# Half-width first gate/up blocks, paired scores and a separate last projection in an attention and gated-unit kernel

## The chip, the cores and the metric

The kernel runs on one core of one Trainium2 chip. The metric is the device time in microseconds of one execution. The core has a matrix engine (TensorE, PE in the profile), a vector engine (DVE), an activation engine (ACT), a general engine (POOL) and SP, which here issues DMAs. Each takes its instructions in order and waits on semaphores. Weight loads of TensorE stand apart as PEld.

## The reference

Everything works on 2048 tokens of width 512 and is in bfloat16. With `xn` the layer norm of `x`:

```python
s = _A_ref(xn, A_k_cache, A_v_cache, A_wq, A_wo)   # 32 heads of 128, 2048 keys, softmax, output projection
g = _silu(_B_ref(xn, B_W_gate, B_W_up, B_W_down))  # relu(gate) * up, inner width 1792, then down to 512
return x + s * g
```

Per head the attention is `q = xn @ wq`, `p = softmax(q k^T / sqrt(128))`, `o = p v`; the heads' outputs, side by side, go through `wo` (4096 to 512).

## The kernel before, in words

Tokens are cut into four quarters Q of 512 (QB = 4) and 16 tiles n of 128 (NT). The head of the kernel normalises the first quarter by hand (`head_ln`): statistics of four tiles on DVE, square root on ACT, norms of tiles 0 and 1 on POOL and of 2 and 3 on DVE, then TensorE transposes each tile into PSUM (`head_transpose`), and ACT (three) and DVE (one) copy them into `xnT`. Before that, twelve dummy matmuls on a zero tile run on TensorE. The first weights, 256 columns of gate and of up, come in SP's queue and ACT's queue; the later ones in SP's.

The gated unit follows by quarters (`emit_gate_up`, `emit_down`): for each of 14 column blocks fc of 128, four gate matmuls and four up matmuls of 512 columns, a relu on ACT (L432), a product on DVE (L438); then the down projection, whose gate value lands in `g_sb`. During the first quarter DVE, POOL and SP normalise and transpose the other quarters (`ln_task`).

PSUM has a ring of three slots of two banks (`ps_r`, `ring_acquire`) and two banks of accumulators (`ps_acc`). `ring_acquire` makes TensorE wait until the slot's last readers are done.

The long part is attention. A block b is one head and one quarter: 128 blocks of 8 pairs. A pair is 2 tiles of 128 keys. For each pair TensorE makes two score matmuls (L582) into one ring slot, ACT takes the exponential of both (L592) into `PT`, and three pairs later (LAG) TensorE multiplies with the values, eight matmuls of 129 columns (L675), the last column being the softmax's sum. At a block's end DVE takes reciprocals (L605) and scales (L612), and SP transposes the result by DMA into `OT_store` (L627). At the first block of each group of four heads, DVE waits for all transposes of the group before (L603).

The order of TensorE's work is written out by hand in a dictionary `plan`. It gives steps of the pair loop extra tiles: at the first pair of a block the query projection of the next head (L515, four matmuls) and one tile of the output projection of the group before (L536, four matmuls); in the last four blocks, which have no next head, two tiles at the first and fifth pair. Steps without extra tiles run score, four values, score, four values. Steps with them run both scores, the extra tiles, eight values.

The last group's projection (`emit_final_tile`, L709) multiplies with the gate on DVE (L717), adds to `x` (L722) and stores. Its tiles for quarters 0 and 1 are in the plan of blocks 126 and 127. After the loop come the four of quarter 2, then the last block's output, which TensorE transposes and ACT copies (L647, L652), then the four of quarter 3.

Of the kernel before, what the change touches and what calls it, by code (L numbers as in the profile page):

```python
# [5 lines left out]
BF16 = mybir.dt.bfloat16  # L6
# [45 lines left out]
def bass_recurrent_scan__mha_block_cached__glu_gated_reglu__prompt_kernel(  # L52
# [51 lines left out]
    with ExitStack() as es:  # L104
# [60 lines left out]
        sem_tl = [newsem(16) for _ in range(QB)]  # L165
        sem_ptr = newsem()
        sem_otc = newsem()
# [29 lines left out]
        with nc.Block() as block:  # L197

            @block.tensor
            def _(_pe_eng):  # L200
# [13 lines left out]
                FCS = [0, min(2, FC), min(8, FC), FC]  # L214
# [24 lines left out]
                load_w(act, Wu_sb, wu_src, sem_wu, 0)  # L239
# [103 lines left out]
                def head_transpose(n, ntok, eng, sem):  # L343
                    tp_ps = ps_r[:, n, :].bitcast(BF16)
# [13 lines left out]
                    ring_tok[n // 2].append(ctok)  # L358

                def head_ln():  # L360
                    st = ln_stats(0)
                    st = ln_stats(1)
                    sq01 = ln_aggr([0, 1], st)
                    st = ln_stats(2)
                    c01 = ln_coef([0, 1], sq01)
                    n0 = ln_norm(pool, sem_nm, 0, c01)
                    n1 = ln_norm(pool, sem_nm, 1, c01)
                    st = ln_stats(3)
                    sq23 = ln_aggr([2, 3], st)
                    c23 = ln_coef([2, 3], sq23)  # L370
                    n2 = ln_norm(dve, sem_ln4, 2, c23)
                    n3 = ln_norm(dve, sem_ln4, 3, c23)
                    head_transpose(0, n0, act, sem_xa)
                    head_transpose(1, n1, act, sem_xa)
                    head_transpose(2, n2, act, sem_xa)
                    head_transpose(3, n3, dve, sem_xt)

# [27 lines left out]

                def emit_gate_up(Q):
                    qs = slice(Q * NQ, (Q + 1) * NQ)
                    par = Q % 2
                    h_tok = None
                    for fc in range(FC):  # L410
                        fs = slice(fc * 128, (fc + 1) * 128)
                        s = ring_acquire()
# [16 lines left out]
                        gk = fc % NSLOT  # L429
                        _wait(act, gtok)  # L430
                        _wait(act, gr_free[gk])
                        rtok = sem_relu.sig(act.activation(gr_sb[gk][:], ps_r[:, gb, :], ACTF.Relu))  # L432
                        _wait(dve, gu_tok)
                        _wait(dve, rtok)
                        if fc == 0:
                            _wait(dve, hT_free[par])
                        h_tok = sem_h.sig(
                            dve.tensor_tensor(hT[par][:, fc, :], gr_sb[gk][:], ps_r[:, gb + 1, :], ALU.mult)  # L438
                        )
                        gr_free[gk] = h_tok  # L440
                        ring_tok[s] = [rtok, h_tok]
                        if Q == 0:
                            ln_task(fc)
# [33 lines left out]
                for _i in range(12):  # L477
                    pe.matmul(ps_acc[:, 0, 0:D], warm[:, 0:128], warm[:], start=True, stop=True)
                head_ln()
                ring_cnt[0] = 2  # L480
# [17 lines left out]
                opg_tok = {}  # L498
                def blk_of(gp):
                    b, p = divmod(gp, NP)  # L500
                    h, Q = divmod(b, QB)
                    return b, h, Q, p

                def emit_M(items):
                    s = ring_acquire()
                    toks = [fn(*args, 2 * s + k) for k, (fn, *args) in enumerate(items)]
                    ring_tok[s] = toks
# [59 lines left out]
                s_slot = {}  # L567

                def open_S_pair(gp):
                    b, h, Q, p = blk_of(gp)  # L570
                    if p == 0:
                        _wait(pe, qt_ready[(h, Q)])
                        if Q == 0:
                            _wait(pe, kt_tok(h))
                    s_slot[gp] = ring_acquire()

                def emit_S_tile(gp, tt):
                    b, h, Q, p = blk_of(gp)
                    qs = slice(Q * NQ, (Q + 1) * NQ)
                    s = s_slot[gp]  # L580
                    t = 2 * p + tt
                    ins = pe.matmul(ps_r[:, 2 * s + tt, :], KT_sb[h % 2][:, t * 128:(t + 1) * 128],  # L582
                                    QT_sb[h % 2][:, qs], start=True, stop=True)
                    if tt == 0:
                        return
# [11 lines left out]
                def emit_norm_bank(b, bank, pvtok):  # L597
# [19 lines left out]
                    if b == NBLK - 1:  # L617
                        emit_last_transposes(hh, Q, ob, bank, tok)
                        return tok
# [3 lines left out]
                    tsem = sem_t[g % 2] if g < NG - 1 else sem_tl[Q]  # L623
                    for jj in range(2):
                        j = 2 * bank + jj
                        tsem.sig(
# [7 lines left out]
                last_ot = {}  # L634

                def emit_last_transposes(hh, Q, ob, bank, tok):
                    pending_last.append((hh, Q, ob, bank, tok))

                def flush_last_transposes():
                    s = ring_acquire()  # L640
                    for k, (hh, Q, ob, bank, tok) in enumerate(pending_last):
                        tp_ps = ps_r[:, 2 * s + k, :].bitcast(BF16)
                        _wait(pe, tok)
                        ins = None
                        for jj in range(2):
                            j = 2 * bank + jj
                            ins = pe.transpose(tp_ps[:, jj * 128:(jj + 1) * 128], Onorm[ob][:, j, :], ident[:])  # L647
                        ptok = sem_ptr.sig(ins)
                        _wait(act, ptok)
                        c0 = Q * NQ + bank * 256  # L650
                        last_ot[bank] = sem_otc.sig(
                            act.copy(OT_store[(NG - 1) % 2][:, hh, c0:c0 + 256], tp_ps[:, 0:256])  # L652
                        )
                    ring_tok[s] = list(last_ot.values())

                pending_last = []

                def emit_PV_tile(gp, tt):
# [3 lines left out]
                    if tt == 0:  # L662
                        if p == 0:
                            if gp == 0:
                                _wait(pe, tok_pool)
                            if Q == 0:
                                _wait(pe, v_tok(h))
                        pe.wait_ge(sem_exp.h, gp + 1)
                    t = 2 * p + tt
                    for j in range(4):  # L670
                        bank = j // 2
                        if t == 0 and j % 2 == 0:
                            _wait(pe, norm_tok[b - 1][bank] if b >= 1 else acc_free[bank])
                        o_ap = ps_acc[:, bank, (j % 2) * 256:(j % 2) * 256 + VW]
                        ins = pe.matmul(o_ap, PT[pb][:, tt, j * 128:(j + 1) * 128], V_sb[vb][:, t, :],  # L675
                                        start=(t == 0 and j % 2 == 0), stop=(t == KT - 1 and j % 2 == 1))
                        if t == KT - 1 and j == 1:
                            tx = sem_pv.sig(ins)
                        if t == KT - 1 and j == 3:
                            ty = sem_pv.sig(ins)  # L680
                    if t == KT - 1:
# [5 lines left out]
                        norm_tok[b] = (ntx, nty)  # L687

# [4 lines left out]

                NFT = len(fin_tmp)
                fin_free = [None] * NFT
                fin_cnt = [0]
                gL = NG - 1

                def emit_final_tile(n, bank):
                    Q, j = divmod(n, 4)  # L700
                    if n == 0:
                        _wait(pe, wo_tok(gL))
                    if j == 0:
                        _wait(pe, (sem_tl[Q], sem_tl[Q].n))
                    if Q == QB - 1:
                        _wait(pe, last_ot[j // 2])
                    ins = None
                    for hh in range(G):
# [3 lines left out]
                    fb = fin_cnt[0] % NFT  # L712
                    fin_cnt[0] += 1
                    _wait(dve, otok)
                    _wait(dve, fin_free[fb])
                    mtok = sem_opa.sig(
                        dve.tensor_tensor(fin_tmp[fb][:], ps_r[:, bank, 0:D], g_sb[:, n, :], ALU.mult))  # L717
                    _wait(dve, mtok)
                    if n == 0:
                        _wait(dve, base_done[NT - 1])  # L720
                    ftok = sem_opa.sig(
                        dve.tensor_tensor(x_sb[:, n, :], x_sb[:, n, :], fin_tmp[fb][:], ALU.add))  # L722
                    fin_free[fb] = ftok
                    if Q == QB - 1 or j % 2 == 1:
                        n0 = n if Q == QB - 1 else n - 1
                        _wait(sp, ftok)
                        sem_out.sig(sp.dma_start(out_t[:, n0:n + 1, :], x_sb[:, n0:n + 1, :]))
                    return mtok

                plan = {}  # L730
                for b in range(NBLK):
# [82 lines left out]
```

## Time and profile before

| what | value |
|---|---|
| median of 3 runs | 1299.38 us (1299.02 to 1300.44) |
| profiled execution, its own time | 1300.44 us |
| its span | 1298.6 us |
| TensorE busy | 1287.6 us |
| ACT busy | 1001.6 us |
| DVE busy | 442.5 us |
| DMA moved | 71.69 MB, 55 GB/s on average |
| exponentials (L592) | 1024, 952.5 us busy |
| value matmuls (L675) | 8192, 784.2 us busy |
| score matmuls (L582) | 2048, 755.1 us busy |

Busy time is the union of the instructions' durations. A matmul's duration holds the time in which its last column drains through the array, so neighbours overlap; how often matmuls start says more than how long each lasts. The span is from the first to the last instruction of the profiled execution, and its own time has 1.8 us around it.

### The profile page before, as it was taken

Reading aid. Unit: us, or ns where it says so; the run is one execution under the profiler, and the core shown is the slowest. Engines: PE = TensorE matmul, PEld = TensorE weight load, DVE = VectorE, ACT = ScalarE, POOL = GpSimd, SP = SyncE. Lnnn points to the kernel's source line nnn. Section 1 sums busy time; section 2 is a strip of 40 time slices with the busy share of each in tenths; the row PEclk is TensorE's granted clock in tenths of the full one; section 3 lists DMA queues with packets and bytes.
Section 4 is the critical chain, followed back from the end, with each engine's and each line's share of the span. In section 5 each row is a group of like instructions: output and inputs, shape, how many; then the busy total and the mean of one; then the engine's idle time right before and its main releaser. Section 6 shows DMA issues by size and latency. Waiting matters only on the chain.

```text
span 1298.6 us, 27683 instructions
## 1 busy us (share of the span) xinstructions
PE 1287.6 (99%) x11968; PEld 835.3 (64%) x11968; DVE 442.5 (34%) x1190; ACT 1001.6 (77%) x1109; POOL 11.5 (1%) x23
## 2 busy tenths in 40 slices
PE   9999999999999999999999999999999999999998
PEld 4444466666666666666666666666666666666665
DVE  6333322222323323323323323323323322334456
ACT  3322399888888888888888888888888888888884
POOL 2000000000000000000000000000000000000000
PEclk9999999999999999999999999999999999999999
DMA  9500112222222322232211322232223211232202
GB/s 259 114 1 1 21 39 47 47 56 42 52 52 54 68 52 54 52 68 53 53 36 34 69 52 54 52 69 54 52 52 53 69 36 33 52 68 54 47 16 73
DMA packets 250999, 71.69 MB, mean 55 GB/s; under 512 B 237824, under 2 KB 250880, under 8 KB 250880
## 3 DMA queue, kind: packets, MB, share of 16 engines
q1 hardware_dynamic: 250064, 69.41, 25.2%
q8 instruction: 95, 1.56, 0.5%
q10 hardware_dynamic: 816, 0.52, 0.1%
q14 instruction: 24, 0.20, 0.1%
HBM read 32.77 MB, written 2.10 MB: 27 GB/s over the span
## 4 chain that ended last, share of the span: by engine, by line
PE 93%; DVE 3%; SPq 2%; DMA 1%; issue 0%; ACT 0%; DVEq 0%
PE ps_acc L675 35%; PE ps_r L582 32%; PE ps_r L515 7%; PE ps_r L536 7%; PE ps_r L422 4%; PE ps_acc L459 4%; PE ps_r L426 4%; DVE Onorm L612 2%; SPq L627 2%; PE ps_r L709 1%; DMA OT_store<-Onorm 1%; DVE rz_sb L605 0%; DMA x_sb<-in_A_x_dram 0%; DVE stats L313 0%; DVE s_acc L561 0%
## 5 line engine op out<-in xcount | busy, mean ns | idle before, releaser
L592 ACT ACTIVATE PT<-ps_r 128x1024 bf16<-128x1024 f32 x1024 | 952.5, 1050 | 179.0 <-PE ps_r L582 179.0
L675 PE MATMUL ps_acc<-V_sb,PT 128*128 128x129 bf16 x8192 | 784.2, 221 | 3.3 <-DVE Onorm L612 1.6
L675 PEld LDWEIGHTS ps_acc<-V_sb,PT 128*128 128x128 bf16 x8192 | 623.1, 98 | 249.3 <-DVE Onorm L612 7.0
L582 PE MATMUL ps_r<-QT_sb,KT_sb 128*128 128x512 bf16 x2048 | 755.1, 380 | 0.0
L605 DVE RECIPROCAL rz_sb<-ps_acc 128x2 f32<-128x2 f32 x256 | 42.3, 165 | 726.7 <-PE ps_acc L675 698.0
L582 PEld LDWEIGHTS ps_r<-QT_sb,KT_sb 128*128 128x128 bf16 x2048 | 195.4, 98 | 1.1 <-DVE QT_sb L526 0.4
L612 DVE TENSOR_SCALAR Onorm<-ps_acc,rz_sb 128x128 bf16<-128x128 f32 x512 | 156.1, 347 | 9.2
L515 PE MATMUL ps_r<-xnT,Wq_sb 128*128 128x512 bf16 x512 | 130.9, 379 | 0.0
L536 PE MATMUL ps_r<-Wo_sb,OT_store 128*128 128x512 bf16 x448 | 114.7, 379 | 0.0
L515 PEld LDWEIGHTS ps_r<-xnT,Wq_sb 128*128 128x128 bf16 x512 | 49.8, 97 | 60.8 <-ACT PT L592 24.2
L526 DVE CAST QT_sb<-ps_r 128x512 bf16<-128x512 f32 x128 | 87.2, 681 | 0.7 <-PE ps_r L515 0.7
L536 PEld LDWEIGHTS ps_r<-Wo_sb,OT_store 128*128 128x128 bf16 x448 | 43.6, 98 | 53.4 <-DMA OT_store<-Onorm 1.2
L432 ACT ACTIVATE gr_sb<-ps_r 128x512 bf16<-128x512 f32 x56 | 33.4, 597 | 54.2 <-PE ps_r L422 54.0
L549 DVE TENSOR_TENSOR s_acc<-s_acc,ps_r 128x512 f32<-128x512 f32 x96 | 66.0, 687 | 13.3 <-PE ps_r L536 1.1
L422 PE MATMUL ps_r<-xnT,Wg_sb 128*128 128x512 bf16 x224 | 57.5, 379 | 0.6 <-DVE xnT L356 0.6
L426 PE MATMUL ps_r<-xnT,Wu_sb 128*128 128x512 bf16 x224 | 57.5, 379 | 0.0
L438 DVE TENSOR_TENSOR hT<-gr_sb,ps_r 128x512 bf16<-128x512 bf16 x56 | 38.4, 687 | 47.2 <-PE ps_r L426 44.4
L459 PE MATMUL ps_acc<-Wd_sb,hT 128*128 128x512 bf16 x224 | 49.0, 379 | 0.0
L465 ACT ACTIVATE sig_sb<-ps_acc 128x512 f32<-128x512 f32 x16 | 9.6, 597 | 38.8 <-PE ps_acc L459 38.8
L422 PEld LDWEIGHTS ps_r<-xnT,Wg_sb 128*128 128x128 bf16 x224 | 21.8, 98 | 26.9 <-ACT xnT L356 0.7
L459 PEld LDWEIGHTS ps_acc<-Wd_sb,hT 128*128 128x128 bf16 x224 | 21.9, 98 | 26.4
L426 PEld LDWEIGHTS ps_r<-xnT,Wu_sb 128*128 128x128 bf16 x224 | 21.9, 98 | 26.4
(36 smaller groups left out, 126.4 us busy)
## 6 DMA issues: line engine op xcount, KB each, us to landing
V_sb<-in_A_v_cache_dram SPq DMA_DIRECT2D x32, 512.0 KB, 5.3
OT_store<-Onorm SPq DMA_TRANSPOSE x508, 2.4
Wq_sb<-in_A_wq_dram SPq DMA_DIRECT2D x32, 128.0 KB, 2.8
Wo_sb<-in_A_wo_dram SPq DMA_DIRECT2D x8, 512.0 KB, 4.2
Wd_sb<-in_B_W_down_dram SPq DMA_DIRECT2D x1, 1792.0 KB, 13.5
Wg_sb<-in_B_W_gate_dram SPq DMA_DIRECT2D x2, 768.0 KB, 9.7
Wu_sb<-in_B_W_up_dram SPq DMA_DIRECT2D x2, 768.0 KB, 10.4
x_sb<-in_A_x_dram SPq DMA_DIRECT2D x3, 512.0 KB, 10.8
```

What stands on the lines that cost most here:

```text
L422: ins = pe.matmul(ps_r[:, gb, :], Wg_sb[:, c, fs], xnT[:, c, qs], start=(c == 0), stop=(c == DC - 1))
L426: ins = pe.matmul(ps_r[:, gb + 1, :], Wu_sb[:, c, fs], xnT[:, c, qs], start=(c == 0), stop=(c == DC - 1))
L459: ins = pe.matmul(ps_acc[:, jb, 0:D], hT[par][:, fc, j * 128:(j + 1) * 128], Wd_sb[:, fc, :], start=(fc == 0), stop=(fc == FC - 1))
L515: ins = pe.matmul(ps_r[:, bank, :], Wq_sb[b][:, c, :], xnT[:, c, qs], start=(c == 0), stop=(c == DC - 1))
L526: etok = sem_qpe.sig(dve.tensor_copy(QT_sb[b][:, qs], ps_r[:, bank, :]))
L536: ins = pe.matmul(ps_r[:, bank, 0:D], OT_store[g % 2][:, hh, n * 128:(n + 1) * 128], Wo_sb[g % 2][:, hh, :], start=(hh == 0), stop=(hh == ...
L549: dve.tensor_tensor(s_acc[:, n, :], s_acc[:, n, :], ps_r[:, bank, 0:D], ALU.add)
L582: ins = pe.matmul(ps_r[:, 2 * s + tt, :], KT_sb[h % 2][:, t * 128:(t + 1) * 128], QT_sb[h % 2][:, qs], start=True, stop=True)
L592: act.activation(PT[pb][:], ps_r[:, 2 * s:2 * s + 2, :], ACTF.Exp, scale=scale)
L605: rztok = sem_rz.sig(dve.reciprocal(rz_sb[:, bank, :, :], z_ap))
L612: dve.tensor_scalar(Onorm[ob][:, j, :], ps_acc[:, bank, base:base + Dh], rz_sb[:, bank, jj, :], None, op0=ALU.mult,)
L675: ins = pe.matmul(o_ap, PT[pb][:, tt, j * 128:(j + 1) * 128], V_sb[vb][:, t, :], start=(t == 0 and j % 2 == 0), stop=(t == KT - 1 and j % ...
```

## The change

Four things differ.

- **First weights.** The first piece of gate and up has three column blocks instead of two, and up's first piece is issued by SP after gate's instead of by ACT.
- **Head.** The norms of tiles 0 and 1 run on DVE. The transposes use the accumulator banks instead of the ring. Three more dummy matmuls follow the first two transposes. Gate and up of column blocks 0 and 1 then run on the first 256 tokens, before the transposes of tiles 2 and 3; column block 2 on the same tokens after them; then the three blocks on the other 256 tokens. The relu and product of these three blocks come when both halves are done.
- **Loop.** Each step issues both scores, then the extra tiles if any, then eight values. The plan is gone: a queue gives one tile of the output projection to the first pair of each block, in the last four blocks too.
- **End.** All 16 tiles of the last group's projection run after the loop, after all DMA transposes of the group, the last block's among them; the path over TensorE's transposes is gone. Results are stored four tiles at a time, at the end two, one and one.

```diff
-                FCS = [0, min(2, FC), min(8, FC), FC]
+                FCS = [0, min(3, FC), min(8, FC), FC]
+                HFC = 3
...
-                load_w(act, Wu_sb, wu_src, sem_wu, 0)
+                load_w(sp, Wu_sb, wu_src, sem_wu, 0)
...
                 def head_transpose(n, ntok, eng, sem):
-                    tp_ps = ps_r[:, n, :].bitcast(BF16)
+                    tp_ps = acc_bf[n % 2]
+                    _wait(pe, acc_free[n % 2])
...
+                def warm_mm(k):
+                    for _i in range(k):
+                        pe.matmul(ps_r[:, 2 * NSLOT - 1, 0:D], warm[:, 0:128], warm[:], start=True, stop=True)
...
                     c01 = ln_coef([0, 1], sq01)
-                    n0 = ln_norm(pool, sem_nm, 0, c01)
-                    n1 = ln_norm(pool, sem_nm, 1, c01)
+                    n0 = ln_norm(dve, sem_ln4, 0, c01)
+                    n1 = ln_norm(dve, sem_ln4, 1, c01)
+                    head_transpose(0, n0, act, sem_xa)
+                    head_transpose(1, n1, act, sem_xa)
+                    warm_mm(3)
                     st = ln_stats(3)
                     sq23 = ln_aggr([2, 3], st)
+                    emit_half(0, range(HFC - 1), xt_ready[0][0:2])
                     c23 = ln_coef([2, 3], sq23)
                     n2 = ln_norm(dve, sem_ln4, 2, c23)
                     n3 = ln_norm(dve, sem_ln4, 3, c23)
-                    head_transpose(0, n0, act, sem_xa)
-                    head_transpose(1, n1, act, sem_xa)
                     head_transpose(2, n2, act, sem_xa)
                     head_transpose(3, n3, dve, sem_xt)
+                    emit_half(0, range(HFC - 1, HFC), [])
+                    emit_half(1, range(HFC), xt_ready[0][2:4])
...
+                def emit_half(k, fcs, toks):
+                    hs = slice(k * 256, (k + 1) * 256)
+                    for fc in fcs:
+                        fs = slice(fc * 128, (fc + 1) * 128)
+                        if k == 0:
+                            if fc == 0:
+                                pe.wait_ge(sem_wg[0].h, 16)
+                            half_slots.append(ring_acquire())
+                        if fc == 0:
+                            _wait_all(pe, toks)
+                        s = half_slots[fc]
+                        for i, W in enumerate((Wg_sb, Wu_sb)):
+                            if k == 0 and fc == 0 and i == 1:
+                                pe.wait_ge(sem_wu[0].h, 16)
+                            ins = None
+                            for c in range(DC):
+                                ins = pe.matmul(ps_r[:, 2 * s + i, hs], W[:, c, fs], xnT[:, c, hs],
+                                                start=(c == 0), stop=(c == DC - 1))
+                            if k == 1:
+                                half_tok[(fc, i)] = (sem_gate if i == 0 else sem_gu).sig(ins)
...
+                        if Q == 0 and fc < HFC:
+                            s = half_slots[fc]
+                            finish_gate_up(Q, fc, s, half_tok[(fc, 0)], half_tok[(fc, 1)])
+                            continue
...
+                def emit_M(h_qp, Q_qp, op_item):
+                    do_qp = h_qp is not None and h_qp < H and (h_qp, Q_qp) not in qt_ready
+                    if not do_qp and op_item is None:
+                        return
                     s = ring_acquire()
...
-                def open_S_pair(gp):
+                def emit_S_pair(gp):
...
+                    s = ring_acquire()
+                    ins = None
+                    for tt in range(2):
+                        t = 2 * p + tt
+                        ins = pe.matmul(ps_r[:, 2 * s + tt, :], KT_sb[h % 2][:, t * 128:(t + 1) * 128],
+                                        QT_sb[h % 2][:, qs], start=True, stop=True)
...
-                    if b == NBLK - 1:
-                        emit_last_transposes(hh, Q, ob, bank, tok)
-                        return tok
...
-                    tsem = sem_t[g % 2] if g < NG - 1 else sem_tl[Q]
...
+                        if hh == G - 1 and Q == QB - 1 and g < NG - 1:
+                            for n in range(NT):
+                                oproj_queue.append((bcount[0] + OPROJ_DELAY, g, n))
...
+                        emit_S_pair(gp)
+                    gq = step - LAG
+                    if gq >= 0:
+                        bq, hq, Qq, pq = blk_of(gq)
+                        if pq == 0:
+                            bcount[0] += 1
+                            op_item = None
+                            if oproj_queue and oproj_queue[0][0] <= bcount[0]:
+                                _, g_, n_ = oproj_queue.pop(0)
+                                op_item = (g_, n_)
+                            emit_M(hq + 1, Qq, op_item)
+                        emit_PV_pair(gq)
+
+                while oproj_queue:
+                    _, g_, n_ = oproj_queue.pop(0)
+                    emit_M(None, None, (g_, n_))
...
+                for n in range(NT):
...
+                    if n == 0:
+                        _wait(pe, t_tok(gL))
+                        _wait(pe, wo_tok(gL))
```

`finish_gate_up` is the relu and product of before's `emit_gate_up`, now a function of its own.

## The prediction

> **What bounds the kernel now.** I read the busy table and the clock row first, then the groups of costly instructions, then the timeline of one block of the long loop, then the timelines of the first 15 us and the last 15 us, because the change touches the head, the order inside the loop and the tail.
>
> ```profile
> PE 1287.6 (99%) x11968; PEld 835.3 (64%) x11968; DVE 442.5 (34%) x1190; ACT 1001.6 (77%) x1109; POOL 11.5 (1%) x23
> PEclk9999999999999999999999999999999999999999
> PE 93%; DVE 3%; SPq 2%; DMA 1%; issue 0%; ACT 0%; DVEq 0%
> L592 ACT ACTIVATE PT<-ps_r 128x1024 bf16<-128x1024 f32 x1024 | 952.5, 1050 | 179.0 <-PE ps_r L582 179.0
> ```
>
> TensorE is the bound, at full clock, and the chain of waits is TensorE for 93%. ACT, the next, sits idle 179 us waiting for scores. So time changes only where TensorE's order opens or closes a gap, or where work stands at an end with TensorE idle.
>
> One block in the timeline (starts and durations; columns: start, duration, instruction):
>
> ```profile
> 601.29 0.60 PE L582 MATMUL ps_r<-QT_sb,KT_sb 128*128 128x512 bf16 x2
> 601.72 1.03 PE L515 MATMUL ps_r<-xnT,Wq_sb 128*128 128x512 bf16 x4
> 602.58 1.03 PE L536 MATMUL ps_r<-Wo_sb,OT_store 128*128 128x512 bf16 x4
> 603.45 0.62 PE L675 MATMUL ps_acc<-V_sb,PT 128*128 128x129 bf16 x8
> 603.90 0.38 PE L582 MATMUL ps_r<-QT_sb,KT_sb 128*128 128x512 bf16 x1
> 604.12 0.39 PE L675 MATMUL ps_acc<-V_sb,PT 128*128 128x129 bf16 x4
> 604.35 0.38 PE L582 MATMUL ps_r<-QT_sb,KT_sb 128*128 128x512 bf16 x1
> ```
>
> A duration holds the pipeline's drain; the price is start to start. Scores cost 0.216 each (601.29 to 601.72 for two), projections 0.216 (0.86 for four), value matmuls 0.057 (0.45 for eight, 0.23 for four). Such a block takes 8.835 us between first reciprocals (601.37 to 610.21).
>
> **The loop's order.** Where a block has no projections in a step, before runs score, 4 values, score, 4 values: 2x0.216+8x0.057 = 0.888. After runs score, score, 8 values. Both forms stand in the rows above, and no alternation costs anything: 0.43+0.45 against 2x(0.22+0.23). The price is 0 within 0.01 a step. Could it stall? A score pair waits for the exponential of three pairs earlier. Exponentials come every 0.92 from the restart at 604.76; counted from there, the eighth pair starts near 5.6 and the exponential that it needs ends near 4.8. The projection step is the tightest (exponential two back, 5.7 against 6.0), and it is ordered scores, projections, values in both kernels. I take 0. Emitting scores earlier signals a finished pair 0.23 earlier, which ACT, idle 1.40 per block, can only use to idle elsewhere.
>
> **Group boundaries.** Every 16 blocks L605 waits for the last transposed outputs of the group. DVE waited 28.7 us for them in 4 of 7 boundaries; from the reciprocals, those stretches of two blocks are 1.32, 0.70, 0.37 and 0.81 over their like: 3.2 us in all. The code is the same after; K's transpose on SP can start up to 0.23 sooner, and arrivals shift. Bounds: none of 7 stalls (-3.2) to 7 at the worst stretch of 1.39 (10.22 less 8.835; +6.5). I take 0, nearest to an unchanged order.
>
> **The head.** These rows tell when work can begin:
>
> ```profile
> 5.77 0.16 DVE L332 SCALAR_TENSOR_TENSOR nmr<-mv,rstd 128x2 f32<-128x2 f32 x1
> 6.04 1.52 POOL L338 TENSOR_SCALAR xn_sb<-x_sb,rstd,nmr 128x512 bf16<-128x512 bf16 x2 [4.36 <-DVE nmr L332]
> 7.38 1.75 ACT L356 COPY xnT<-ps_r 128x512 bf16<-128x512 bf16 x3 [0.23 <-PE ps_r L350]
> 7.60 0.73 DVE L338 TENSOR_SCALAR xn_sb<-x_sb,rstd,nmr 128x512 bf16<-128x512 bf16 x2
> 9.36 1.02 PE L422 MATMUL ps_r<-xnT,Wg_sb 128*128 128x512 bf16 x4 [0.56 <-DVE xnT L356]
> 14.54 1.03 PE L422 MATMUL ps_r<-xnT,Wg_sb 128*128 128x512 bf16 x4
> ```
>
> The first two norms move from POOL (0.76 each) to DVE (0.41, starts 0.32 apart): from 5.98 they end at 6.39 and 6.71. Transposes follow 0.06 later and take 0.38, then ACT's copies of 0.59, one behind the other: 6.90 to 8.07. Half gate/up starts at 8.16 instead of 9.36, with 256 columns at half of 0.216, 0.108 each. Queued behind: DVE's statistics of the fourth tile now follow the norms (6.7 to 7.3), and ACT's square root waits behind the copies until 8.07, so the third and fourth norms end at 9.27 and 9.6. Sixteen half matmuls run to 9.9, eight transposes to 10.35 (56 ns each), eight half matmuls to 11.2 while the copies end at 10.98, and 24 halves to 13.85. Three dummies (0.65) fit between 7.15 and 8.16. Column block 3 starts at 13.85, where before's starts at 14.54: -0.7.
>
> Weights: the queue table gives gate's first 256 KB 6.0 from issue to landing (7.7), up's on ACT's queue 6.9 (8.6). After moves 384 KB each, both in SP's queue ahead of the rest. Gate is wanted at 8.16, up at 8.6. Bounds: up at 8.2 (no wait) to 9.6, one more 384 KB behind it at the 350 GB/s of this stretch (a wait of 1.0, which moves the transposes with it). So -0.7, from -0.9 to +0.3. SP's later issues shift by one issue of 0.5; x of the second quarter still lands near 13.5, under the same bytes.
>
> The Trainium skill, "Trainium Kernel Development and Optimization", section Key Constraints, says that DMAs from several engines' queues share the same 16 DMA engines and that issuing from several only saves issue time; by it the move from ACT's queue is worth nothing either way, which is the -0.7.
>
> **The tail, where the price lies.** Before keeps TensorE busy to the end: it puts 13 projection tiles into the last four blocks, 8 of them final, and turns the last block with TensorE.
>
> ```profile
> 251.22 0.90 PE L675 MATMUL ps_acc<-V_sb,PT 128*128 128x129 bf16 x8
> 1247.52 0.17 DVE L605 RECIPROCAL rz_sb<-ps_acc 128x2 f32<-128x2 f32 x1 [4.42 <-PE ps_acc L675]
> 1278.13 6.31 SPq L627 DMA_TRANSPOSE OT_store<-Onorm  x4
> 1290.13 0.68 DVE L717 TENSOR_TENSOR fin_tmp<-ps_r,g_sb 128x512 bf16<-128x512 f32 x1
> 1291.19 0.68 DVE L717 TENSOR_TENSOR fin_tmp<-ps_r,g_sb 128x512 bf16<-128x512 f32 x1
> 1296.15 0.42 DVE L722 TENSOR_TENSOR x_sb<-x_sb,fin_tmp 128x512 bf16<-128x512 bf16 x1
> ```
>
> After, in before's clock: up to 1247.52 nothing differs but the head. Blocks 124 to 126 hold one tile each. Such blocks stand early in the loop (the 251.22 row): 8.25 each, with 0.27 in which the values wait for the norm of the block before (0.90 against 0.62). Block 127 is 0.43+0.86+0.27+0.46, four steps of 0.888 and three value groups of 0.456: 6.94. Its first reciprocal: 1247.52+24.76+6.94 = 1279.2 (before 1286.56; nine tiles have left).
>
> Then the last four DMA transposes: first issue 0.85 after the reciprocal (1277.28 to 1278.13), three more 1.26 apart, 2.4 to land: 6.9. With the hiccups of the last blocks it was 6.9 to 8.6; I take 7.5, and 0.1 to the matmul. TensorE has only the left-over tile (0.86) meanwhile, so finals start at 1286.8 after 6.6 idle. Sixteen finals: TensorE needs 0.86 each, DVE 1.06 each (1290.13 to 1291.19, the product and the addition), so DVE bounds: first product 1.06 after the start (0.86 and the drain), last 15x1.06 later, 1.14 to the last addition's end: 1304.9. Before's last addition ends at 1296.57 and the span 2.03 later; the same gives 1306.9. The tail costs +8.3 with a warm TensorE.
>
> **The clock after the idle.** Trace:
>
> ```profile
> 1.19 4.84 PE L478 MATMUL ps_acc<-warm 128*128 128x512 bf16 x12 [1.19 <-DVE warm L233]
> 1295.00:1298.60 3.60, 0.00 (x0) 0.00 (x0) 1.51 (x4) 0.00 (x0) 0.00 (x0) 1.00 0.32 109
> ```
>
> From rest, ten matmuls come 0.427 apart before the rate doubles. An idle TensorE still had a granted clock of 1.00 some 4 us after its last matmul (window row: last 1.00 is the clock). 6.6 idle is shown nowhere: the price lies between 0 (stays warm) and all 64 matmuls at 0.427 (27.3 for 16.9, +10.4). Nearest is the start from rest: ten slow matmuls put the first products at 1.9, 3.6 and 4.9 instead of 1.06, 2.12 and 3.18; from there DVE bounds: +1.7. I take it.
>
> The Trainium skill, "TensorE: Matmul & The Clock Gate", section Why this matters for your kernels, warns against TensorE gaps of over about 3 us, after which it returns to half clock. It speaks against this tail, though the row of 1.00 after 4 us does not yet bear it out; by the rule the sum would be +9.3, by that row alone +7.6.
>
> **Sum**: -0.7 +0 +0 +8.3 +1.7 = +9.3. The profiled execution (span 1298.6, 1300.44 around it) becomes 1307.9 and 1309.7. It is 1.06 over the median of three, 1299.38, so the median becomes 1308.7.
>
> **Rivals.**
> - TensorE stays warm (the 4 us row speaks for it, the slow start against): +7.6, 1307.0. Chance 0.22.
> - The head gains nothing because up's weights come at 9.6 (for: 384 KB instead of 256; against: one queue in order): +10.3, 1309.7. Chance 0.12.
> - The boundaries become the loss: all seven stall (4 did, by transposes landing late): +9.3+6.5, 1315.2; halfway 1312. Chance 0.08.
> - Faster: pairing the scores saves TensorE time in all 897 steps without projections. It must save 9.3/897 = 10.4 ns a step to break even; twice that would give 1290. The 0.43+0.45 against 0.89 speaks against it. Chance 0.04, of which half is within 0.2%.
> - The forecast itself: 0.54.
>
> Range: from a warm start with the earliest landing (7.6-0.6) and 1.9 of the boundaries gone, +5.1, to the forecast with a landing of 8.6 (+1.1) and two more boundaries at 1.39, +13: 1304.5 to 1312.4. Measurement can tell 0.2%, 2.6 us, from no change. Same: half of the fast rival and a little for the best end, 0.04; faster 0.02.
>
> **What would show it.** Right: blocks of 8.83 with score pairs; column block 3 near 13.9; no TensorE work for over 6 us after the leftover tile; finals 1.06 apart on DVE, the first ones 1.7; a granted clock under 1 there. Wrong: steps unlike 0.888, finals that start within 4 us, or boundary waits far from 28.7.

## The result, and the profile after

The changed kernel takes 1308.76 us (median of 4 runs, 1308.0 to 1309.35), the kernel before 1299.91 in the same comparison (1299.02 to 1301.79). The ratio is 1.0066, with a 95% interval of 1.0048 to 1.0083: slower by 8.85 us. Run again with the experiments below it took 1308.43 beside 1299.23 (1.0072, 1.0055 to 1.0089). The profiled execution has a span of 1307.3 and a time of 1309.07.

The page of the changed kernel, for the lines that were shown of before:

```profile
PE 1290.2 (99%) x11991; PEld 840.0 (64%) x11991; DVE 443.1 (34%) x1192; ACT 1000.5 (77%) x1107; POOL 10.0 (1%) x21
PEclk9999999999999999999999999999999999999999
PE 94%; DVE 4%; issue 1%; SPq 1%; DMA 1%; ACT 0%; DVEq 0%
```

The shares hardly differ. A page of 40 slices of 33 us each can't show what happened: most of the loss lies in one stretch of 7 us. Three marks in the two timelines place it (all in us from the start of each span):

| mark | before | after | lost from mark to mark |
|---|---|---|---|
| first reciprocal of block 0 | 167.47 | 166.90 | -0.57 |
| first reciprocal of block 123 | 1247.52 | 1247.22 | +0.27 |
| end of the span | 1298.62 | 1307.27 | +8.95 |

So the head gained 0.57, the loop lost 0.27, and the tail lost 8.95: together 8.65. The tail in the timeline of the changed kernel (weight loads and value matmuls left out):

```profile
1278.91 1.03 PE L587 MATMUL ps_r<-Wo_sb,OT_store 128*128 128x512 bf16 x4
...
1285.94 15.32 PE L768 MATMUL ps_r<-Wo_sb,OT_store 128*128 128x512 bf16 x64 [6.01 <-issue]
1287.85 0.69 DVE L773 TENSOR_TENSOR fin_tmp<-ps_r,g_sb 128x512 bf16<-128x512 f32 x1 [5.27 <-PE ps_r L768]
...
1289.21 0.69 DVE L773 TENSOR_TENSOR fin_tmp<-ps_r,g_sb 128x512 bf16<-128x512 f32 x1 [0.21 <-PE ps_r L768]
...
1290.28 0.68 DVE L773 TENSOR_TENSOR fin_tmp<-ps_r,g_sb 128x512 bf16<-128x512 f32 x1
...
1291.34 0.68 DVE L773 TENSOR_TENSOR fin_tmp<-ps_r,g_sb 128x512 bf16<-128x512 f32 x1
...
1304.07 0.68 DVE L773 TENSOR_TENSOR fin_tmp<-ps_r,g_sb 128x512 bf16<-128x512 f32 x1
```

After the leftover tile TensorE is idle for 6.01 us, until the last transposes have landed. Then come sixteen products on DVE, the first ones 1.36 and 1.07 apart, the others 1.06. The windows of the same stretch (columns: window, its length, busy time and instruction count of PE, PEld, DVE, ACT and POOL, granted clock, DMA share, GB/s) show why the first are slower:

```profile
1279.00:1285.30 6.30, 0.93 (x6) 0.20 (x3) 3.44 (x9) 0.00 (x0) 0.00 (x0) 1.00 0.10 21
1285.30:1288.70 3.40, 2.76 (x7) 1.02 (x8) 0.82 (x2) 0.00 (x0) 0.00 (x0) 0.50 0.00 0
1288.70:1302.00 13.30, 12.56 (x58) 5.45 (x56) 12.67 (x26) 0.00 (x0) 0.00 (x0) 1.00 0.24 82
```

The granted clock fell to half, 5.3 us after the leftover tile's last matmul had ended, just before TensorE was needed again.

One block of the loop, start to start: in these rows two scores take 0.44 and eight values 0.46.

```profile
602.68 0.62 PE L694 MATMUL ps_acc<-V_sb,PT 128*128 128x129 bf16 x8
603.14 0.60 PE L631 MATMUL ps_r<-QT_sb,KT_sb 128*128 128x512 bf16 x2
603.58 0.62 PE L694 MATMUL ps_acc<-V_sb,PT 128*128 128x129 bf16 x8
```

Blocks with two extra tiles take 8.847 us after and 8.835 before; those with one take 8.267 and 8.254.

The head:

```profile
6.07 0.74 DVE L336 TENSOR_SCALAR xn_sb<-x_sb,rstd,nmr 128x512 bf16<-128x512 bf16 x2
7.05 1.07 ACT L355 COPY xnT<-ps_acc 128x512 bf16<-128x512 bf16 x2 [1.52 <-PE ps_acc L349]
8.26 0.60 PE L403 MATMUL ps_r<-xnT,Wg_sb 128*128 128x256 bf16 x4 [0.36 <-ACT xnT L355]
13.95 1.03 PE L477 MATMUL ps_r<-xnT,Wg_sb 128*128 128x512 bf16 x4
```

Half matmuls begin at 8.26 and column block 3 at 13.95, against 14.54 before.

### The profile page after: what moved, and what is told of

It is laid out like the page before. It is cut to its first block, busy times and chain, and to the rows that moved or that the text cites. A ratio compares the mean times of both kernels' runs of the same rounds, so it can differ in the third digit from the quotient of the medians.

```text
span 1307.3 us, 27724 instructions
## 1 busy us (share of the span) xinstructions
PE 1290.2 (99%) x11991; PEld 840.0 (64%) x11991; DVE 443.1 (34%) x1192; ACT 1000.5 (77%) x1107; POOL 10.0 (1%) x21
## 4 chain that ended last, share of the span: by engine, by line
PE 94%; DVE 4%; issue 1%; SPq 1%; DMA 1%; ACT 0%; DVEq 0%
PE ps_acc L694 35%; PE ps_r L631 33%; PE ps_r L566 7%; PE ps_r L587 7%; PE ps_acc L500 4%; PE ps_r L481 4%; PE ps_r L477 4%; DVE Onorm L659 2%; SPq L670 1%; DVE fin_tmp L773 1%; DVE rz_sb L652 0%; PE ps_r L403 0%; DMA OT_store<-Onorm 0%; PE ps_r L768 0%; DMA x_sb<-in_A_x_dram 0%
## 5 line engine op out<-in xcount | busy, mean ns | idle before, releaser
L694 PEld LDWEIGHTS ps_acc<-V_sb,PT 128*128 128x128 bf16 x8192 | 551.8, 98 | 248.7 <-DVE Onorm L659 6.8
L694 PE MATMUL ps_acc<-V_sb,PT 128*128 128x129 bf16 x8192 | 640.7, 221 | 2.8 <-DVE Onorm L659 0.7
L631 PE MATMUL ps_r<-QT_sb,KT_sb 128*128 128x512 bf16 x2048 | 609.7, 380 | 0.0
L631 PEld LDWEIGHTS ps_r<-QT_sb,KT_sb 128*128 128x128 bf16 x2048 | 159.3, 98 | 1.1 <-DVE QT_sb L577 0.4
L481 PE MATMUL ps_r<-xnT,Wu_sb 128*128 128x512 bf16 x212 | 54.4, 379 | 0.0
L477 PE MATMUL ps_r<-xnT,Wg_sb 128*128 128x512 bf16 x212 | 54.4, 379 | 0.0
```

The source lines that it names most:

```text
L477: ins = pe.matmul(ps_r[:, gb, :], Wg_sb[:, c, fs], xnT[:, c, qs], start=(c == 0), stop=(c == DC - 1))
L481: ins = pe.matmul(ps_r[:, gb + 1, :], Wu_sb[:, c, fs], xnT[:, c, qs], start=(c == 0), stop=(c == DC - 1))
```

## The experiments

Theory: the tail is the loss. Its parts are the wait for the last block's DMA transposes, the clock that falls in that wait, and sixteen products on DVE with nothing beside them. The head gives some 0.6 back, and pairing the scores costs 12 ns a block. The main rival: pairing, or the order of the tiles in the loop, is the loss. The tail of each run is compared by one number, from the first reciprocal of block 123 to the end of the span (51.1 before, 60.05 after).

**The tail back.** The changed kernel's head, before's plan and end, paired scores:

```diff
                         open_S_pair(gp)
                         emit_S_tile(gp, 0)
-                        if items:
-                            emit_S_tile(gp, 1)
+                        emit_S_tile(gp, 1)
                     if items:
                         emit_M(items)
                     emit_PV_tile(gq, 0)
-                    if gp < TOTP and not items:
-                        emit_S_tile(gp, 1)
                     emit_PV_tile(gq, 1)
```

> The changed kernel's head and its paired scores, with the order of the tail taken from the kernel before: projection tiles in the last four blocks, the last block turned by TensorE. Theory (the tail is the whole loss, +8.3 to +9.9; the head gives about 0.6; pairing costs 12 ns a block, 1.5 us in all): the span is within 1 us of the kernel before's, 1298.5 to 1300.5, and no granted clock under 1 near the end. Rival (paired scores are the loss, the tail only a part): at least 3 us slower than before, 1302 or more. Last reciprocal to span end 12.0 as in the kernel before, by the theory.

1298.32 against 1297.99 for the kernel before, ratio 1.0003 (0.9993 to 1.0012). Last mark: 1296.4 - 1245.43 = 51.0, as before. The clock is 1.00 to the end. The rival falls: with before's tail the loss is gone. The span came out 2 us under the expected interval, and the last reciprocal to the end was 12.05, as expected. What differed was the boundary waits, none here against 2.6 in the first profile of before; they are taken up below.

**Pairing alone.** The same diff on the kernel before.

> The kernel before, with both scores issued before the values in every step and nothing else changed. Theory: blocks of two extra tiles go from 8.835 to 8.847 us (7 steps of 1.7 ns), about +1.4 us over the loop if the boundary waits stay, 1300 to 1302. Rival (pairing is free, and the 12 ns come from something else, such as the accumulator banks or the queue of tiles): blocks stay at 8.835. Second rival (signalling the last scores of a head earlier shortens the boundary waits): the waits of the reciprocals for transposes fall under the 28.7 us of before by the 1.2 us by which the four long stretches shrank in the changed kernel.

1299.60 against 1297.99, ratio 1.0010 (1.0001 to 1.0020). Blocks take 8.847 and 8.267, as in the changed kernel. So pairing itself costs 12 ns a block. Spread over the seven steps without extra tiles that is 1.7 ns a step; 123 blocks make 1.5 us. The first rival (something else makes the 12 ns) falls. The starts of single matmuls show where it goes. Two scores take 432.5 ns in either order. The eight values take 457.5 ns in a row and 455.9 as two groups of four, and one start stands out: the sixth value matmul starts 60 to 61 ns after the fifth in all 826 such steps of the changed kernel between 200 and 1240 us, while the other starts among the values and to the next score are 55 to 58 ns apart. The fifth is the first on the step's second tile of keys; in the order of before a score stands at that place. Why the start after it is late isn't settled. The waits for transposes were fewer, 13.8 us on DVE against 28.7, but runs that share before's order differ by as much, so the second rival isn't shown.

**TensorE kept busy through the wait.** In the changed kernel:

```diff
                 gL = NG - 1
+                sd = ring_acquire()
+                for _i in range(26):
+                    pe.matmul(ps_r[:, 2 * sd, 0:D], warm[:, 0:128], warm[:], start=True, stop=True)
```

> The changed kernel with 26 dummy matmuls of 512 columns (5.6 us) after the leftover projection tile, so that TensorE works through the wait for the last transposes. Theory (6 us of idle let the clock fall to half, which delays the products by 1.2 us): no granted clock of 0.5 before the last matmul, the first products on DVE 1.06 apart from the first on, the span from the first last-group matmul to the end 21.4 minus 1.2, 20.2; the time 1.2 us under the changed kernel's, 1307.5. Rival (DVE bounds the finals anyway and absorbs a slow start): no change, 1308.8. If the dummies run over the transposes' landing the start is late by up to 0.5.

The timeline of this run:

```profile
1278.23 5.78 PE L753 MATMUL ps_r<-warm 128*128 128x512 bf16 x26
1278.30 4.92 SPq L670 DMA_TRANSPOSE OT_store<-Onorm  x4
1284.40 5.77 PE L771 MATMUL ps_r<-Wo_sb,OT_store 128*128 128x512 bf16 x25 [0.40 <-issue]
1285.46 0.69 DVE L776 TENSOR_TENSOR fin_tmp<-ps_r,g_sb 128x512 bf16<-128x512 f32 x1 [4.42 <-PE ps_r L771]
1286.53 0.68 DVE L776 TENSOR_TENSOR fin_tmp<-ps_r,g_sb 128x512 bf16<-128x512 f32 x1
1287.59 0.68 DVE L776 TENSOR_TENSOR fin_tmp<-ps_r,g_sb 128x512 bf16<-128x512 f32 x1
```

The products are 1.06 apart from the first. The clock stays at 1.00 until 1300.48, 2.1 us after the last final matmul. From block 127's first reciprocal (1277.46) to the last product (1301.38) is 23.92, against 25.08 in the changed kernel (1278.99 to 1304.07): 1.16 less, the expected 1.2. The start is the same, 6.94 after that reciprocal. The last mark is 58.89. The time is 1306.44, ratio 1.0064 (1.0049 to 1.0079); the changed kernel's interval overlaps it, so for 1 us the trace decides, not the ratio. DVE doesn't absorb the slow start: the rival falls.

**The last block turned by TensorE, finals still after the loop.**

```diff
-                            plan.setdefault((LB + k // 4, 4 * (k // 2 % 2)), []).append((emit_oproj_tile, g, n))
-                for Q in range(QB - 2):
-                    for j in range(4):
-                        plan.setdefault((LB + 2 + Q, 4 * (j // 2)), []).append((emit_final_tile, 4 * Q + j))
+                            if k < QB:
+                                plan[(LB + k, 0)] = [(emit_oproj_tile, g, n)]
...
-                for n in range(NT - 8, NT - 4, 2):
+                emit_M([(emit_oproj_tile, NG - 2, NT - 1)])
+                for n in range(0, NT - 4, 2):
```

This stands on the first experiment's kernel.

> The changed kernel, but the last block is turned by TensorE as in the kernel before; all sixteen last-group tiles still follow the loop and the leftover tile. It takes away the wait for the last block's DMA transposes and so the idle. Theory (of the tail's loss, the wait of 6 us and the slow clock of 1.2 are the larger part; sixteen products in a row on DVE at 1.06, with nothing beside them, are the rest): 6 to 7.2 us under the changed kernel, 1301.5 to 1302.8, still 1.5 to 3 over the kernel before. Rival (sixteen tiles outside the loop are the loss, by DVE's 17 us, and the wait is hidden behind them): under 3 us gained, 1306 or more.

1302.47, ratio 1.0034 (1.0022 to 1.0045); the last mark is 54.36, so 5.69 of the tail's 8.95 went and 3.26 stay. That is a little less than the 6 to 7.2 expected. By the times it is 4.48 slower than its own runs of before, where the changed kernel was 8.85 and 9.20 slower than its own; but before came out between 1297.99 and 1299.91 from one comparison to the next, so the marks are the better measure. DVE's timeline shows what the remainder is:

```profile
1277.94 0.17 DVE L647 RECIPROCAL rz_sb<-ps_acc 128x2 f32<-128x2 f32 x1 [3.39 <-PE ps_acc L717]
...
1279.39 0.67 DVE L591 TENSOR_TENSOR s_acc<-s_acc,ps_r 128x512 f32<-128x512 f32 x1
1280.10 0.69 DVE L603 TENSOR_TENSOR s_acc<-s_acc,g_sb 128x512 f32<-128x512 f32 x1
1280.83 0.69 DVE L606 TENSOR_TENSOR x_sb<-x_sb,s_acc 128x512 bf16<-128x512 bf16 x1
1281.43 0.68 DVE L759 TENSOR_TENSOR fin_tmp<-ps_r,g_sb 128x512 bf16<-128x512 f32 x1
```

With the wait gone, the leftover tile's three additions are next: the first product stands behind them on DVE, 3.5 us after the reciprocal, with finals already done in PSUM. Then DVE bounds at 1.06 a tile. The rival (sixteen tiles outside the loop are the loss) is right only for 3.26. The tail's 8.95 is 3.26 of DVE's work at the end, 1.16 of slow clock by the busy tail, and the rest, 4.53, is put down to the wait itself.

**The changed kernel again.**

> The changed kernel once more, for its time beside the same runs of the kernel before as the others. Theory: from the reciprocal of block 123 to the end of the span 60.0 us, as in its first profile (the kernel before: 51.1), if the last transposes land 6.9 after the last block's reciprocal, up to 1.7 more if they land late; clock at half from about 5.4 after the last matmul. Time 1306 to 1308.8, 8 to 9.5 over the kernel before.

1308.43; last mark 60.4. Here the clock fell earlier and stayed low longer:

```profile
1282.60:1289.40 6.80, 3.97 (x10) 1.46 (x11) 1.48 (x3) 0.00 (x0) 0.00 (x0) 0.50 0.04 10
1289.40:1302.00 12.60, 11.89 (x55) 5.17 (x53) 12.19 (x25) 0.00 (x0) 0.00 (x0) 1.00 0.27 90
```

The first three products came 1.70 and 1.12 apart, and the slow clock cost 1.55 by the same reckoning (third product 2.82 after the first, warm 2.12, and the first 0.85 late). It fell about 3.1 us after the last matmul's end, not 5.3.

**The head alone**, on the kernel before:

> The kernel before with the new head alone (half-width first blocks, norms on DVE, three dummies, both first weights in SP's queue). Theory: column block 3 starts at 13.85 to 14.1 instead of 14.3 to 14.5, the first reciprocal comes 0.6 us earlier, and as TensorE is busy from there on, the time falls by 0.6: about 1297.4 where the kernel before has 1298.0. Rival (the time won is given back, as column blocks 3 and 4 wait for weights, or at the boundaries): less than 0.2 gained.

1297.79 against 1299.23, ratio 0.9988 (0.9979 to 0.9998). Column block 3 starts at 14.00, the first reciprocal at 166.73: 0.74 before the first profile's 167.47, 0.53 before the pairing run's 167.26, which has the old head. The 0.6 is passed on whole. The time fell by 1.44, which is more; the boundary waits, 0.57 us in this profile and 2.6 in the first one of before, could make the difference, but that isn't shown.

**Without the three dummies:**

```diff
-                    warm_mm(3)
```

> The new head alone without the three dummies between the first transposes and the first half matmuls. Theory (TensorE rests only 1 us there, and a rest of 4 us still had the full clock): the half matmuls stay 0.109 apart and column block 3 starts where it does with them, within 0.15 us. Rival (the clock falls without them): half matmuls 0.21 apart for some us, column block 3 at 15 or later.

Column block 3 starts at 14.22, half matmuls are 0.109 apart from the first, and from their first (8.32) to column block 3 it takes 5.90, as with the dummies (8.10 to 14.00). The start is 0.22 later, a little over the 0.15 allowed, for a reason that isn't the dummies: the first eight transposes, which stand before them. The rows without the dummies, then with them:

```profile
6.48 0.87 PE L352 MATMUL ps_acc<-ident,xn_sb 128*128 128x128 bf16 x8
```

```profile
6.47 0.63 PE L352 MATMUL ps_acc<-ident,xn_sb 128*128 128x128 bf16 x8 [0.84 <-DVE xn_sb L339]
```

Without the dummies most of these transposes started 107 ns apart, until the rate rose at 7.1 us; with them, 55 to 67. From the first transpose to the first half matmul it takes 1.84 without the dummies and 1.63 with them. In the busy tail and in the run with the last block on TensorE, which have the dummies, the transposes also came 107 ns apart, and it takes 1.84 and 1.89. So this one execution shows no use of the dummies, and its 0.22 is not their price.

**Up's first weights in ACT's queue:**

```diff
-                load_w(sp, Wu_sb, wu_src, sem_wu, 0)
+                load_w(act, Wu_sb, wu_src, sem_wu, 0)
```

> The new head alone, with up's first weights (384 KB) issued from ACT's queue as in the kernel before. Theory (a piece in the second queue shares each DMA engine with the larger pieces that follow in SP's): up lands 0.7 to 1.5 later than the 7.6 to 7.9 of the one queue, at 8.6 to 9.4, and the first up matmul, wanted at 8.7, waits 0 to 0.7; column block 3 is late by as much. Rival (the queue makes no difference, as all share the same engines): up lands within 0.3 of 7.9 and nothing moves.

TensorE's timeline of this run, then the DMA issues of this run, then those of the new head alone (columns: KB each, us to landing):

```profile
8.77 0.61 PE L406 MATMUL ps_r<-xnT,Wg_sb 128*128 128x256 bf16 x4 [0.96 <-DMA Wg_sb<-in_B_W_gate_dram]
9.65 0.61 PE L406 MATMUL ps_r<-xnT,Wu_sb 128*128 128x256 bf16 x4 [0.27 <-DMA Wu_sb<-in_B_W_up_dram]
```

```profile
Wg_sb<-in_B_W_gate_dram SPq DMA_DIRECT2D x1, 384.0 KB, 7.1
Wu_sb<-in_B_W_up_dram ACTq DMA_DIRECT2D x1, 384.0 KB, 7.9
```

```profile
Wg_sb<-in_B_W_gate_dram SPq DMA_DIRECT2D x1, 384.0 KB, 5.0
Wu_sb<-in_B_W_up_dram SPq DMA_DIRECT2D x1, 384.0 KB, 5.7
```

Both pieces come about 2 us later, not up's alone: gate at 8.72 instead of 6.70, up at 9.60 instead of 7.81. Column block 3 starts at 15.12, later than with the old head. The nine profiles with this head and one queue have gate at 6.38 to 6.96 and up at 7.56 to 8.20, so the single profile of this run lies well outside their spread. So the one queue carries the head's gain. The theory named the right direction but missed gate. The Trainium skill, "DMA: Bandwidth & Descriptors", section Issuing engines are not separate DMA queues, says that DMAs from several engines interleave on the same 16 DMA engines and that issuing from several only saves issue time. For throughput nothing here speaks against that; for the moment at which the first piece is complete, these profiles do, by 1.1 us of the head.

**The boundary waits taken away**, on the kernel before:

```diff
-    NON = G * QB
+    NON = G * QB + 4
...
-                    if bank == 0 and b % (G * QB) == 0 and g >= 1:
+                    if bank == 0 and b % (G * QB) == 4 and g >= 1:
                         _wait(dve, t_tok(g - 1))
```

> The kernel before with 20 instead of 16 buffers for the scaled outputs, so that DVE's wait for the last group's transposes can stand at the fifth block of a group instead of the first. Theory (the four long stretches of blocks, 3.2 us in the first profile and 0.6 to 2.0 in later ones, come from this wait, and are what varies from run to run): DVE no longer waits for transposes at the reciprocals, all seven stretches are like their neighbours, the time falls by 1 to 3 us and spreads less. Rival (the output projection of the group, whose TensorE wait stands one block later, takes the delay over): no gain, and TensorE waits for transposes at the first projection tile of a group.

1297.61 against 1299.44, ratio 0.9988 (0.9979 to 0.9997), over a range of 1.0 us in 11 runs instead of before's 2.8 in 22. The waits of the first reciprocals in the kernel before, in this run, and the projection's wait in this run:

```profile
DVE rz_sb L605 <- DMA OT_store<-Onorm: 28.7, 4, 7.4
```

```profile
DVE rz_sb L605 <- PE ps_acc L675: 723.1, 127, 6.1
PEld ps_r L536 <- DMA OT_store<-Onorm: 0.7, 2, 0.4
```

DVE no longer waits for transposes, and only 0.12 us of boundary is left, where the first projection tile of a group waits: the rival holds for that much. The boundary waits of the other profiles, summed over the seven boundaries, are 2.6 (before), 1.45 (after), 1.1 (after again), 0.8 (pairing alone), 0.5 (last block on TensorE), 0.57 (head alone), 0.94 (without the dummies, and with ACT's queue) and 0 (tail back, busy tail). They differ between kernels whose order around the boundary is the same.

**Head, buffers, and additions on POOL:**

```diff
+                    eng, sem = (pool, sem_fp) if n % 2 == 0 else (dve, sem_opa)
...
-                        dve.tensor_tensor(x_sb[:, n, :], x_sb[:, n, :], fin_tmp[fb][:], ALU.add))
+                        eng.tensor_tensor(x_sb[:, n, :], x_sb[:, n, :], fin_tmp[fb][:], ALU.add))
```

> The kernel before with the new head, the 20 buffers, and every second addition of the last projection on POOL, beside DVE's products. Theory: 0.6 from the head, 1 to 3 from the boundaries, and about 0.8 at the end (from the last eight products 1.06 apart to 0.88, TensorE's 0.86 bounding): 2.4 to 4.4 under the kernel before, 1294 to 1296. Rival (POOL's addition is slow, or slows DVE's beside it): no gain at the end, products still 1.06 apart or more.

1297.14 against 1299.44, ratio 0.9984 (0.9975 to 0.9993): 2.30 less, just short of the 2.4 expected at the least. The end gained nothing:

```profile
1288.88 1.27 DVE L760 TENSOR_TENSOR fin_tmp<-ps_r,g_sb 128x512 bf16<-128x512 f32 x2
1289.63 1.15 POOL L766 TENSOR_TENSOR x_sb<-x_sb,fin_tmp 128x512 bf16<-128x512 bf16 x1 [0.96 <-DVE fin_tmp L760]
1290.18 0.88 DVE L766 TENSOR_TENSOR x_sb<-x_sb,fin_tmp 128x512 bf16<-128x512 bf16 x1
1290.99 1.27 DVE L760 TENSOR_TENSOR fin_tmp<-ps_r,g_sb 128x512 bf16<-128x512 f32 x2
```

Two tiles take 2.11 (1288.88 to 1290.99), 1.06 each as before. DVE's addition, 0.42 alone, takes 0.88 while POOL's of 1.15 runs beside it: the rival was right. The Trainium skill, "GPSIMD Engine Reference", section 1. Specifications, says that VectorE and GpSimd share their SBUF interfaces and that DVE instructions with two SBUF inputs contend; the 0.88 agrees.

**The same, and each block's first values bank by bank:**

```diff
+                    if pq == 0:
+                        emit_PV_tile(gq, 0, (0, 1))
+                        emit_PV_tile(gq, 1, (0, 1), False)
+                        emit_PV_tile(gq, 0, (2, 3), False)
+                        emit_PV_tile(gq, 1, (2, 3), False)
+                        continue
```

> The same with the first pair's eight value matmuls of each block taken bank by bank (two key tiles into the first accumulator bank, then two into the second) instead of tile by tile. Theory (in the 17 blocks with one extra tile, the second bank's norm is what the values wait for, 0.27 us a block): two more value matmuls before that wait, 2x0.057 = 0.11 a block, 17 blocks, 1.9 us under the run without it; blocks of 8.254 become 8.14, those of 8.835 stay. Rival (the wait is for the first bank): blocks stay at 8.25.

1295.25 against 1299.44, ratio 0.9970 (0.9959 to 0.9982), and 1.89 under the run without it. The values of the first pair, without and with it:

```profile
250.63 0.90 PE L718 MATMUL ps_acc<-V_sb,PT 128*128 128x129 bf16 x8
```

```profile
249.20 0.79 PE L718 MATMUL ps_acc<-V_sb,PT 128*128 128x129 bf16 x8
```

0.11 less in each such block: they take 8.138 instead of 8.253, those of 8.835 stay (8.837). This version is 4.2 us faster than the kernel before; the changed one is 8.85 slower, each against its own runs of it.

## Why the prediction was right

The forecast was 1308.7 and the median is 1308.76, but a part of that closeness is luck: pairing and the boundaries, both taken at 0, came out at +1.5 and -1.2 and nearly cancel, and the boundary waits vary as much among profiles of one order of the loop (2.6 against 0.57 and 0.94). Against the profiled execution (span 1307.9 forecast, 1307.3 measured) the terms stand so:

| term | forecast | measured | from |
|---|---|---|---|
| head | -0.7 | -0.57 | first reciprocal; 13.95 where 13.85 was worked out |
| pairing | 0 | +1.5 | 12 ns in each of 123 blocks, shown by pairing alone |
| boundaries | 0 | -1.2 | 1.45 instead of 2.6 |
| tail, warm | +8.3 | +7.8 | 8.95 less 1.16 |
| clock | +1.7 | +1.16 | busy tail; 1.55 in the second profile |
| sum | +9.3 | +8.65 | the span; the rounded terms make 8.7 |

The sign and the place were right for the reason given: the wait for the last transposes with TensorE idle, finals bounded by DVE at 1.06, and the clock. The tail back takes the loss away, and the two tail experiments split it.

Four sizes were off. The landing was taken at 7.5 after the reciprocal, the middle of 6.9 and 8.6; it was 6.9. The clock was costed at ten slow matmuls from rest, a count of one execution (in the other profiles six to all eleven starts of these dummies were slow); the slow stretch had begun 0.66 us before the finals did and was 3.4 us long, so fewer were slow. In the second profile it began 3 us before and was twice as long, and cost 1.55; the forecast of 1.7 was near the upper of the two. Pairing was bounded by 0.01 a step, which over 897 steps is 9 us; the row's 10 ns of resolution couldn't show the 1.7 ns that it cost. Before's own trace had it in its single starts: in its 118 projection steps between 200 and 1240 us eight values follow one another too, and there too the sixth starts 60 to 61 ns after the fifth. And the boundary waits were held unchanged, when they vary from profile to profile; their sum in before was also overstated, at 3.2 where it is 2.6, because the block after the first boundary has two extra tiles while the one of the boundary has one, so 0.58 of the 1.32 was no wait. The worst stretch of 1.39, used for the rival and for the top of the range, counts one block and leaves out that the next one was 0.58 short; as two blocks it is 0.81, so both bounds were too high.

The head's gain came out near its forecast, but one premise was wrong: the move of up's first weights to SP's queue was taken to be worth nothing, and the run with ACT's queue shows that 1.1 us of the head hangs on it.

Of the rivals, the warm clock is refuted by the granted clock of 0.50, late weights by up's landing at 7.9, the boundaries as a loss by 1.45, and the gain by pairing by the sign of its 12 ns.

The range, 1304.5 to 1312.4, held the time.

## What to carry to other kernels

When work is moved out of a loop that one engine bounds, its own duration cancels; what costs is the wait that it then stands behind, and the engine that bounds it alone (here DVE at 1.06 a tile, where TensorE needs 0.86). Put independent tiles under the last transfer, and turn the last block on the engine that is idle anyway. A wait that varies between executions, such as one that covers a whole group of transfers, hides differences of a microsecond; a few more buffers took it away here and made the times comparable as well.

## What the runs showed of the hardware

- The granted clock fell to 0.50 at 5.3 and at 3.1 us after the last matmul before the wait in two executions of the same kernel, and stayed there for 3.41 and 6.83 us, one and two times the same length; the full clock after it lasted 17.07 us in both, five times that length. In the tail with dummies it fell only 2.1 us after the last final matmul.
- Two DMAs of 384 KB in one queue landed at 6.38 to 6.96 and 7.56 to 8.20 us in nine profiles; with the second in another queue they landed at 8.72 and 9.60 in one.
- Of eight value matmuls in a row, the sixth started 60 to 61 ns after the fifth and the others 55 to 58 ns apart, in the paired steps of the changed kernel.
- A DVE addition of two bfloat16 tiles in SBUF took 0.88 us instead of 0.42 while POOL did the same kind of addition in 1.15.
